# Attention on TensorE: hash masks of two blocks on quarters of the rows, four score slots, and small steps moved to ScalarE

## Chip, cores and metric

The kernel runs on one core of one Trainium2 chip. The metric is the device time of one execution in microseconds (us), as the median of several runs. TensorE is called PE, VectorE DVE, ScalarE ACT, GpSimd POOL and the SyncE queue SP.

## What is computed

Hashed attention over 4 batches of 8 heads (768 tokens, 64 dimensions), followed by a feed-forward layer. All inputs are float32. Cut to what matters:

```python
q_bits = (einsum('bhsd,dk->bhsk', q, proj) > 0)      # 6 bits; k_bits likewise
mask = q_bucket[:, :, :, None] == k_bucket[:, :, None, :]
scores = where(mask, q @ k.T / sqrt(64), -1e9)
attn = exp(scores - max(scores))
attn = attn / (sum(attn) + 1e-9)
x = (attn @ v) -> (3072, 512)                        # heads side by side
h = x @ w_in                                         # 512 -> 2048
out = (h * erf(softplus(h))) @ w_out                 # 2048 -> 512
```

## The kernel before

Attention takes the heads in 16 pairs; the two heads of a pair, called `ab` 0 and 1, lie on SBUF partitions 0 to 63 and 64 to 127. A pair has 12 score blocks: `n` runs over four steps (two halves of 384 queries, and for each two groups of keys), `c` over three tiles of 128 keys. A block is one PSUM tile `st` of two banks, one for each head. `score` (L543) fills it in two parts: first the mask, a bf16 product of the hash bits `qb` and `kb` (7 rows that hold bits and a constant, the other rows of the 64 are zero), then the float32 product of `k` and `q` on top of it. The mask adds 0 where all bits agree and a huge negative number elsewhere, so that the exponential gives 0 there. Both parts use 64 rows of the array for each head, so the two heads stand side by side. In the trace a float32 matmul is two records, a bf16 one is one.

`exponential` (L581, ACT) reads a block out of PSUM into SBUF (`e_even` for the first half of the queries, `e_odd` in `area` for the second). There are three slots of two banks for score blocks (`big`, L433): block 3 of a pair can start when the exponential of block 0 has ended, and so on.

`weigh` (L632, PE) multiplies by `v`: for each half of the queries 12 matmuls of 128 rows by 64 columns, the two heads on two halves of the columns, accumulated into a tile `av` of one bank. Half 0 and half 1 have a tile and a pool of their own (`psum_v` and `misc`). `leave` (L700, ACT) copies `av` to `x`. A further column of `e_even` that holds 1.0 gives in `av` the plain sum of `v`; `leave_plain` (L710, DVE) multiplies it by 2^-100 into `ev`, the small term that is added to `x` later.

Behind the last `weigh` of a pair stand on PE `bits_of` (L834: hash bits of the pair after the next, on four quarters of 32 columns, tile `bits`) and `divisor` (L670: column sums of the exponentials of the pair before, which DVE has added up in `sum_keys`; it writes beside the bits, in the second bank of the same tile). ACT takes the signs of the bits (`sign_of`, L853, tile `sg`) and the sums (`keep_divisor`, L695). DVE multiplies the rows of k's bits in `sg` by a weight (`weigh_bits`, L862); POOL sends `sg` to DRAM (`leave_bits`) and fetches it back into `both` with two DMAs (`place_bits`, L876). The sums go to DRAM and back as 12 values on each partition, DVE adds a constant and inverts them (`invert`, L741), they are spread over the partitions by DMA, and DVE makes `(x + ev) * r` (`normalise`, L767).

Beside all this DVE and ACT decode the two weight matrices of the feed-forward layer (`square_high` and `keep_normal` on ACT, `move_bits`, `mask_bits`, `add_rest` on DVE), and ACT sums squares of `q` and `k` (`measure`, L660).

The order of the work is made when the program is built. Each step is an `Op` with an engine, an estimated cost, a rank and the steps that it comes after; `arrange` (L120) lists them greedily. For PE the chain is written out by hand (L905 to L944): `score` x4, `weigh` x4, `bits_of`, `divisor`, for each pair. The waits between engines are not written in the kernel: the framework sets them, from the tiles that instructions read and write.

The feed-forward layer (L1201 on) follows with the same engines: seven products instead of eight at each of two levels, and a gate built of sigmoids and a tanh.

Of the kernel before, what the change touches and what calls it, by code (L numbers as in the profile page):

```python
# [63 lines left out]
P = 128  # L64
# [132 lines left out]
def kernel(  # L197
# [32 lines left out]
    dram = ctx.enter_context(tc.tile_pool(name="dram", bufs=2, space=bass.MemoryType.DRAM))  # L230
    misc = ctx.enter_context(tc.tile_pool(name="misc", bufs=1, space=PSUM))
    small = ctx.enter_context(tc.tile_pool(name="small", bufs=3))
    QR = 32
# [7 lines left out]
    sgn = const.tile([P, 1], F32, name="sgn")  # L241
    tiny2 = const.tile([P, 1], F32, name="tiny2")
    cq = const.tile([P, len(GATE_S) + 1], F32, name="cq")
    w_in_sb = const.tile([P, NK, DFF], F32, name="w_in_sb")
# [53 lines left out]
    nc.vector.memset(sgn, -(2.0**-27))  # L298
    nc.vector.memset(tiny2, TINY * TINY)
    for j, c in enumerate([b for _, b, _ in GATE_S] + [GATE_BIAS]):  # L300
        nc.vector.memset(cq[:, j : j + 1], c)

    def bank(name):
        return misc.tile([P, 512], F32, name=name, tag="bank")

# [114 lines left out]
    def attention():  # L420
        NS = NPAIR * 4
        with (
# [17 lines left out]
            e_even = ep.tile([P, NE, 2, HS + 1], F32, name="e_even")  # L440
            nc.vector.memset(e_even[:, :, :, HS : HS + 1], 1.0)
            e_odd = area[:, 0 : NE * S].rearrange("p (n a c) -> p n a c", n=NE, a=2)
# [82 lines left out]
            def add_rest(n):  # L525
# [15 lines left out]
                )  # L541

            def score(n, c, parts=((0, "b"), (1, ""))):  # L543

                i, half, g = n // 4, n // 2 % 2, n % 2
                d = pairs[i]
                cols = slice(half * HS, (half + 1) * HS)
                keys = slice((g * GC + c) * P, (g * GC + c + 1) * P)
                if ("st", n, c) in d:
                    parts = ((1, "b"),)  # L550
                else:
                    d["st", n, c] = big("st")
                st = d["st", n, c]
                for part, src in parts:
                    for ab in range(2):
                        rows = slice(ab * D, ab * D + D)
                        nc.tensor.matmul(  # L557
                            out=st[:, ab, 0:HS],
                            lhsT=d["k" + src][rows, keys],
                            rhs=d["q" + src][rows, cols],  # L560
                            start=(part == 0),
                            stop=(part == 1),
                        )
# [68 lines left out]
            def weigh(n):  # L632
                half, g = n // 2 % 2, n % 2
                d = pairs[n // 4]
                if g == 0:
                    d["av", half] = bank("av") if half else psum_v.tile([P, 512], F32, name="av", tag="av")
                w = HS + 1 - half
# [57 lines left out]
            def keep_divisor(i):  # L695
                d = pairs[i]
                d["z"] = home(i, "z")
                nc.scalar.copy(out=d["z"], in_=d.pop("z_ps"))

            def leave(h):  # L700
# [6 lines left out]
                x = d["x"][half] if i == NPAIR - 1 else d["x"][:, cols]  # L707
                nc.scalar.copy(out=x, in_=d["av", half][:, 0:HS])

            def leave_plain(i):  # L710

                d = pairs[i]
                d["ev"] = small.tile([P, 1], F32, name="ev", tag="ev")
                nc.vector.tensor_scalar(
                    out=d["ev"],
                    in0=d["av", 0][:, HS : HS + 1],
                    scalar1=EPS,
                    scalar2=None,
                    op0=ALU.mult,
                )  # L720
# [20 lines left out]
            def invert(i):  # L741
                d = pairs[i]
                zc = d["zc"]
                nc.vector.tensor_scalar(
                    out=zc, in0=zc, scalar1=S * EPS, scalar2=None, op0=ALU.add
                )
                nc.vector.reciprocal(out=zc, in_=zc)

# [18 lines left out]
            def normalise(i):  # L767
# [36 lines left out]
            pairs[0] = fetch(0, load, quick=True)  # L804
            warm = bank("warm")
            for n in range(WARM):
# [55 lines left out]
            def weigh_bits(i):  # L862

                nc.vector.tensor_scalar(
                    out=sg[D:P, :],
                    in0=sg[D:P, :],
                    scalar1=weight_q[D:P, 0:1],
                    scalar2=None,
                    op0=ALU.mult,
                )  # L870
# [5 lines left out]
            def place_bits(i):  # L876
# [3 lines left out]
                for n, what in enumerate(("qb", "kb")):  # L880
                    d[what] = both[i % 2][:, n, :]
                for ab in range(2):
                    nc.gpsimd.dma_start(
                        out=both[i % 2][ab * D : ab * D + NBIT + 1, :, :].rearrange(
                            "r w (h c) -> r (w h) c", h=2
                        ),
                        in_=bd[:, ab, 0 : NBIT + 1, :].rearrange("n r c -> r n c"),
                    )

# [18 lines left out]
            for i in range(NPAIR):  # L908
# [8 lines left out]
                if i == NPAIR - 2:  # L917
                    order.append(("divisor", i))
            slots = []
            for what, n in order:  # L920
                free = slots[-3] if len(slots) >= 3 else ()
                if what == "score":
                    i = n // 4
                    after = (("double_first",) if i == 1 else ("place_bits", i),)
                    for c in range(GC):
                        free = slots[-3] if len(slots) >= 3 else ()
                        pe(score, (n, c), 0.82 if n or c == 2 else 0.17, after + free)
                        slots.append((("exponential", n, c),))
                elif what == "bits":
                    pe(bits_of, (n,), 0.80 if n > 1 else 1.44, (("start_pair", n),) + free)  # L930
                    slots.append((("sign_of", n),) if n > 1 else (("place_first",),))
                elif what == "divisor":
                    if n != NPAIR - 3:
                        free = ()
                        slots[-1] += (("keep_divisor", n),)
                    else:
                        slots.append((("keep_divisor", n),))
# [34 lines left out]
            for i in range(NPAIR - 1):  # L972
# [3 lines left out]
                    "ACT",  # L976
                    0.48,
                    (0, 4 * i + 6, -1),
                    (("divisor", i), ("spread", i - 2)),
                )  # L980
            for h in range(NH):
                i = h // 2
                op(leave, (h,), "ACT", 0.48, (0, 2 * h, -2), (("weigh", 2 * h + 1), ("send", i - 3)))
                if h % 2 == 0:
                    op(leave_plain, (i,), "DVE", 0.15, (0, 2 * h, 0), (("weigh", 2 * h + 1),))
            for i in range(NPAIR):
                n = 4 * i
                if i:
# [15 lines left out]
                    else:  # L1004
                        op(sign_of, (i,), "ACT", 0.6, (0, n - 6, 9), (("bits_of", i), ("leave_bits", i - 1)))
                        op(weigh_bits, (i,), "DVE", 0.33, (0, n - 6, 1), (("sign_of", i),))
                        op(leave_bits, (i,), "POOL", 0.7, (0, n - 6, 2), (("weigh_bits", i),), late=4.0, far=True)
# [3 lines left out]
                            "POOL",  # L1011
                            1.2,
                            (0, n - 6, 3),
# [16 lines left out]
                op(gather, (i,), "SP", 0.35, (0, n, 1), (("spread", i),), late=4.5, far=True)  # L1030
                op(invert, (i,), "DVE", 0.4, (0, n + 8, 3), (("gather", i),))
                op(ungather, (i,), "SP", 0.35, (0, n, 2), (("invert", i),), late=3.0, far=True)
# [8 lines left out]
                )  # L1041
                op(normalise, (i,), "DVE", 1.02, (0, n + 8, 4), (("widen", i), ("leave", 2 * i + 1)))
                op(send, (i,), "SP", 0.35, (0, n, 4), (("normalise", i),), late=2.2)
# [59 lines left out]
    def general():  # L1103

        with (
# [4 lines left out]
            tc.tile_pool(name="row", bufs=4) as small,  # L1110
            tc.tile_pool(name="psum", bufs=1, space=PSUM) as psum,
        ):

            def big(name):
# [86 lines left out]
    def feed_forward(check, late):  # L1201
        again = late is None
        with (
# [5 lines left out]
            tc.tile_pool(name="ps_f", bufs=1, space=PSUM) as ps_f,  # L1209
            tc.tile_pool(name="ps_l", bufs=1, space=PSUM) as ps_l,  # L1210
        ):
            NTILE = NT // T
            NP = NTILE * NC4
# [619 lines left out]
```

## Time and profile before

| what | value |
|---|---|
| median of 3 runs | 904.84 us (904.79 to 905.12) |
| the profiled execution | 904.72 us, of which 902.9 us from the first to the last instruction |
| granted PE clock | 0.998 of full speed |
| busy: PE, DVE, ACT, POOL | 99%, 74%, 62%, 6% of the span |
| attention on PE | to 313.5 us; the feed-forward layer from there |
| one pair of heads, steady | 19.17 us: 12 score blocks 9.84, `weigh` 7.90, `bits_of` and `divisor` 1.43 |
| busy in such a pair: PE, DVE, ACT | 19.17, 18.43, 15.31 us |

A timeline line reads: start and duration in us, engine, line of the kernel, operation, written tile, tiles read, shapes, and how many records are merged in it. "64*128" in a matmul's shape is the part of the array that it uses, rows by columns. A matmul's recorded duration is longer than the time after which the next one on the same place can start, since they are pipelined.

### The profile page before, as it was taken

The numbers are of one execution on the slowest core, as the hardware profiler recorded it, in microseconds if no ns is written. First come the engines' busy times: TensorE is split into PE (matmuls) and PEld (weight loads), VectorE is DVE, ScalarE is ACT, GpSimd is POOL, SyncE is SP. The second block draws the span as 40 slices with busy tenths as digits, with TensorE's granted clock in tenths as the row PEclk, the third lists the DMA queues.
The fourth block names the chain that finished last, engine by engine and source line by source line (L and its number), as shares of the span: only waits on it lengthen the run. The fifth ranks groups of instructions, "written<-read, shape, count | busy, mean of one in ns | idle before, by whom it ended". The sixth has DMA issues, their size and how long they took to land.

```text
span 902.9 us, 12780 instructions
## 1 busy us (share of the span) xinstructions
PE 894.3 (99%) x5016; PEld 670.9 (74%) x5016; DVE 668.5 (74%) x837; ACT 563.3 (62%) x808; POOL 57.9 (6%) x95
## 2 busy tenths in 40 slices
PE   9999999999999999999999999999999999999997
PEld 5455554455544588888888888888888888888886
DVE  5999999999999879995666556666776666655652
ACT  6788888788886668855645455545655555545520
POOL 1211211111110000000000001000100010000000
PEclk9999999999999999999999999999999999999999
DMA  9547655667551322202231013211421122111211
GB/s 228 149 128 183 200 166 142 196 173 195 154 157 60 101 89 65 82 36 70 59 106 58 14 49 103 82 36 47 105 83 36 36 74 78 35 36 57 63 68 50
DMA packets 65156, 86.82 MB, mean 96 GB/s; under 512 B 34364, under 2 KB 47772, under 8 KB 65088
## 3 DMA queue, kind: packets, MB, share of 16 engines
q1 hardware_dynamic: 56528, 63.81, 24.8%
q0 software_dynamic: 8112, 21.66, 8.6%
q8 instruction: 41, 0.67, 0.3%
q10 hardware_dynamic: 448, 0.46, 0.2%
q14 instruction: 27, 0.22, 0.1%
HBM read 64.67 MB, written 17.30 MB: 91 GB/s over the span
## 4 chain that ended last, share of the span: by engine, by line
PE 99%; DVE 0%; issue 0%; ACT 0%; DVEq 0%
PE M L1361 32%; PE X L1248 29%; PE st L557 17%; PE av L642 14%; PE M L1248 3%; PE bits L845 1%; PE bits L687 1%; PE warm L807 0%; PE bits L377 0%; PE z_ps L687 0%; DVE e L1288 0%; DVE h L1270 0%; ACT both L390 0%; DVE u L1396 0%; DVE norms L1754 0%
## 5 line engine op out<-in xcount | busy, mean ns | idle before, releaser
L1288 DVE SCALAR_TENSOR_TENSOR e<-w,e 128x1024 f32<-128x1024 f32 x144 | 173.7, 1220 | 8.4 <-ACT w L1282 3.9
L1248 PE MATMUL X<-area,w_in_sb 128*128 128x256 f32 x680 | 160.6, 379 | 0.0
L1282 ACT ACTIVATE w<-h,cq 128x1024 f32<-128x1024 f32 x144 | 155.6, 1136 | 0.1
L557 PE MATMUL st<-q,k 64*128 64x384 f32 x768 | 155.1, 482 | 0.0
L1270 DVE TENSOR_TENSOR h<-X,h 128x512 f32<-128x512 f32 x65 | 44.8, 689 | 144.4 <-PE X L1248 144.4
L1248 PEld LDWEIGHTS X<-area,w_in_sb 128*128 128x128 f32 x680 | 129.2, 190 | 17.6
L1361 PE MATMUL M<-w_out_sb,h 128*128 128x256 f32 x576 | 141.1, 379 | 0.0
L1248 PE MATMUL X<-area 128*128 128x256 f32 x520 | 122.8, 379 | 0.0
L1361 PEld LDWEIGHTS M<-w_out_sb,h 128*128 128x128 f32 x576 | 109.4, 190 | 14.9
L1266 ACT COPY h<-X 128x512 f32<-128x512 f32 x85 | 49.3, 580 | 111.4 <-PE X L1248 111.3
L1248 PEld LDWEIGHTS X<-area 128*128 128x128 f32 x520 | 98.8, 190 | 13.4
L1278 ACT ACTIVATE e<-h,cq 128x1024 f32<-128x1024 f32 x48 | 55.1, 1148 | 85.9 <-DVE h L1270 85.8
L1361 PE MATMUL M<-wt,S 128*128 128x256 f32 x384 | 95.1, 379 | 0.0
L557 PEld LDWEIGHTS st<-q,k 64*128 64x128 f32 x768 | 68.8, 187 | 29.7 <-issue 27.2
L630 DVE TENSOR_TENSOR area<-area 128x1536 f32<-128x1536 f32 (+1 forms) x46 | 79.2, 1723 | 7.5 <-ACT area L584 6.3
L1361 PEld LDWEIGHTS M<-wt,S 128*128 128x128 f32 x384 | 73.0, 190 | 9.9
L584 ACT ACTIVATE e_even<-st 128x768 f32<-128x768 f32 x96 | 70.6, 822 | 0.4 <-PE st L557 0.3
L584 ACT ACTIVATE area<-st 128x768 f32<-128x768 f32 x90 | 68.0, 817 | 0.0
L642 PE MATMUL av<-e_even,v 128*64 128x385 f32 x384 | 65.6, 490 | 0.0
L557 PE MATMUL st<-both 64*128 64x384 bf16 x384 | 63.5, 323 | 0.3 <-ACT both L390 0.3
L1303 DVE TENSOR_TENSOR h<-h,e 128x1024 f32<-128x1024 f32 x48 | 57.9, 1220 | 4.6 <-ACT e L1299 4.6
L642 PE MATMUL av<-area,v 128*64 128x384 f32 x360 | 60.6, 486 | 0.0
(129 smaller groups left out, 976.8 us busy)
## 6 DMA issues: line engine op xcount, KB each, us to landing
wt<-wt SPq DMA_DIRECT2D x24, 768.0 KB, 4.2
raw<-in_w_out_dram POOLq DMA_DIRECT2D x16, 512.0 KB, 4.2
raw<-in_w_in_dram POOLq DMA_DIRECT2D x14, 512.0 KB, 4.6
v<-in_v_dram SPq DMA_DIRECT2D x32, 192.0 KB, 4.6
q<-in_qkT_dram SPq DMA_DIRECT2D x30, 192.0 KB, 4.2
k<-in_qkT_dram SPq DMA_DIRECT2D x30, 192.0 KB, 4.7
r<-rd SPq DMA_DIRECT2D x30, 192.0 KB, 3.7
xs<-x SPq DMA_DIRECT2D x15, 384.0 KB, 3.0
```

The source lines that it names most:

```text
L557: nc.tensor.matmul(out=st[:, ab, 0:HS], lhsT=d["k" + src][rows, keys], rhs=d["q" + src][rows, cols], start=(part == 0), stop=(part == 1),)
L584: nc.scalar.activation(out=e[:, :, 0:HS], in_=st[:, :, 0:HS], func=AF.Exp, scale=scale)
L630: nc.vector.tensor_tensor(out=into, in0=one, in1=two, op=ALU.add)
L642: nc.tensor.matmul(out=d["av", half][rows, 0:w], lhsT=d["v"][:, g * GC + c, rows], rhs=e[:, ab, 0:w], start=(g == 0 and c == 0), stop=(g = ...
L1248: nc.tensor.matmul(out=d[where][:, u, :], lhsT=a[:, kc, f : f + P], rhs=b[:, kc, :], start=(first and u == 0 and kc == 0), stop=(last and ...
L1266: nc.scalar.copy(out=quarter(p, q), in_=st[p][where])
L1270: nc.vector.tensor_tensor(out=h, in0=st[p][where], in1=h, op=ALU.add)
L1278: nc.scalar.activation(out=s, in_=unit(p, v), func=AF.Sigmoid, bias=cq[:, n : n + 1])
L1282: nc.scalar.activation(out=q, in_=unit(p, v), func=AF.Sigmoid, scale=GATE_S[j][0], bias=cq[:, j : j + 1])
L1288: nc.vector.scalar_tensor_tensor(out=s, in0=st[p].pop(("q", v, j)), scalar=GATE_S[j][2], in1=s, op0=ALU.add, op1=ALU.mult,)
L1303: nc.vector.tensor_tensor(out=h, in0=h, in1=st[p].pop(("s", v)), op=ALU.mult)
L1361: nc.tensor.matmul(out=banks[name][:, sub, :], lhsT=a[:, u, sub * P : (sub + 1) * P], rhs=b[:, u, :], start=(c == 0 and k == 0), stop=(c = ...
```

## The change

From the third pair on, the masks of two neighbouring blocks are made together (`mask`, new). The hash bits are laid out four times, on rows 0, 32, 64 and 96 (`place_bits` issues four DMAs where it issued two). For blocks 0 and 1, 2 and 3, up to 8 and 9 of a pair, four bf16 matmuls of 32 rows by 128 columns run on the four quarters, two for each block; the float32 parts follow. Blocks 10 and 11 stay as they were.

Score blocks have four slots: three as before (`big`) and one of two banks in `psum_v` with the tag `side`, which serves blocks 3 and 7 of a pair and then `av`. `av` is now one tile of two banks, `avs`, whose half 0 and half 1 are the two halves of the queries. The pool `misc` is opened only in the later phases.

`weigh_bits` goes from DVE to ACT. The extra column of `e_even` holds 2^-100 instead of 1.0, so `av` gives the small term itself; ACT copies it to `ev` ahead of `leave` of half 0, and both `leave` add it as a bias. `normalise` becomes a plain product. The divisors' constant is a bias in `keep_divisor`, and `invert` has only the reciprocal. The planner's costs and conditions are rewritten to match.

```diff
@@ mask (new) and score @@
+            SIDE = (3, 7)
+            QUARTERS = tuple(range(0, 10, 2))
+            def slot_of(n, c):
+                if place(n, c)[1] in SIDE:
+                    return psum_v.tile([P, 2, 512], F32, name="st", tag="side")
+                return big("st")
+            def mask(n, c):
...
+                for m in range(2):
...
+                    st = d["st", n, c] = slot_of(n, c)
+                    for ab in range(2):
+                        rows = slice(ab * D + m * QR, ab * D + (m + 1) * QR)
+                        nc.tensor.matmul(
+                            out=st[:, ab, 0:HS],
+                            lhsT=d["kb"][rows, keys],
+                            rhs=d["qb"][rows, cols],
+                            start=True,
+                            stop=False,
+                        )
...
@@ weigh @@
-                    d["av", half] = bank("av") if half else psum_v.tile([P, 512], F32, name="av", tag="av")
+                    if not half:
+                        d["avs"] = psum_v.tile([P, 2, 512], F32, name="av", tag="side")
+                    d["av", half] = d["avs"][:, half, :]
@@ keep_divisor @@
-                nc.scalar.copy(out=d["z"], in_=d.pop("z_ps"))
+                nc.scalar.activation(
+                    out=d["z"], in_=d.pop("z_ps"), func=AF.Identity, bias=least[:, 0:1]
+                )
@@ leave, leave_plain @@
-                nc.scalar.copy(out=x, in_=d["av", half][:, 0:HS])
-            def leave_plain(i):
...
+                if half == 0:
+                    d["ev"] = small.tile([P, 1], F32, name="ev", tag="ev")
+                    nc.scalar.copy(out=d["ev"], in_=d["av", 0][:, HS : HS + 1])
+                nc.scalar.activation(
+                    out=x, in_=d["av", half][:, 0:HS], func=AF.Identity, bias=d["ev"][:, 0:1]
+                )
@@ invert, normalise, weigh_bits @@
-                nc.vector.tensor_scalar(
-                    out=zc, in0=zc, scalar1=S * EPS, scalar2=None, op0=ALU.add
-                )
...
-                    nc.vector.scalar_tensor_tensor(
-                        out=x, in0=x, scalar=d["ev"][:, 0:1], in1=r, op0=ALU.add, op1=ALU.mult
-                    )
+                    nc.vector.tensor_tensor(out=x, in0=x, in1=r, op=ALU.mult)
...
+                nc.scalar.activation(
+                    out=sg[D:P, :], in_=sg[D:P, :], func=AF.Copy, scale=weight_q[D:P, 0:1]
+                )
@@ the planner @@
+                        if i > 1 and at in QUARTERS:
+                            pe(mask, (n, c), 0.22, ready + free_of(at in SIDE, at + 1 in SIDE))
+                        if i > 1 and at <= QUARTERS[-1] + 1:
+                            cost = 0.655
...
-                    if n % 2 == 0:
-                        after += (("leave", h - 2), ("leave_plain", (h - 2) // 2))
-                    pe(weigh, (n,), 2.0, after)
+                    if n % 4 == 0:
+                        after += free_of(True)
+                        side.append((("leave", h), ("leave", h + 1)))
+                    pe(weigh, (n,), 1.98, after)
```

In the changed kernel `mask` is L569, the rest of a score block L591, `weigh` L678, `divisor` L723, `keep_divisor` L734, the copy to `ev` L748, `leave` L749 and `weigh_bits` L889.

More of the change, by code (lines that the diff above doesn't have):

```diff
@@ L230 @@
     dram = ctx.enter_context(tc.tile_pool(name="dram", bufs=2, space=bass.MemoryType.DRAM))
-    misc = ctx.enter_context(tc.tile_pool(name="misc", bufs=1, space=PSUM))
+    single = []
     small = ctx.enter_context(tc.tile_pool(name="small", bufs=3))
@@ L242 @@
     tiny2 = const.tile([P, 1], F32, name="tiny2")
+    least = const.tile([P, 1], F32, name="least")
     cq = const.tile([P, len(GATE_S) + 1], F32, name="cq")
@@ L299 @@
     nc.vector.memset(tiny2, TINY * TINY)
+    nc.vector.memset(least, S * EPS)
     for j, c in enumerate([b for _, b, _ in GATE_S] + [GATE_BIAS]):
@@ L303, in bank @@
     def bank(name):
-        return misc.tile([P, 512], F32, name=name, tag="bank")
+        return single[-1].tile([P, 512], F32, name=name, tag="bank")
     WP = 512
@@ L440, in attention @@
             e_even = ep.tile([P, NE, 2, HS + 1], F32, name="e_even")
-            nc.vector.memset(e_even[:, :, :, HS : HS + 1], 1.0)
+            nc.vector.memset(e_even[:, :, :, HS : HS + 1], EPS)
             e_odd = area[:, 0 : NE * S].rearrange("p (n a c) -> p n a c", n=NE, a=2)
@@ L541, in add_rest, with place @@
                 )
+            SIDE = (3, 7)
+            QUARTERS = tuple(range(0, 10, 2))
+            def place(n, c):
+                return n // 4, n % 4 * GC + c
+            def slot_of(n, c):
[3 more added lines that the diff above has]
+            def mask(n, c):
+                i, at = place(n, c)
+                d = pairs[i]
+                for m in range(2):
+                    n, c = 4 * i + (at + m) // GC, (at + m) % GC
+                    half, g = n // 2 % 2, n % 2
+                    cols = slice(half * HS, (half + 1) * HS)
+                    keys = slice((g * GC + c) * P, (g * GC + c + 1) * P)
+                    st = d["st", n, c] = slot_of(n, c)
[8 more added lines that the diff above has]
+                        )
             def score(n, c, parts=((0, "b"), (1, ""))):
@@ L549, in score @@
                 if ("st", n, c) in d:
-                    parts = ((1, "b"),)
+                    parts = ((1, "b" if i == 0 else ""),)
                 else:
-                    d["st", n, c] = big("st")
+                    d["st", n, c] = slot_of(n, c)
                 st = d["st", n, c]
@@ L707, in leave @@
                 x = d["x"][half] if i == NPAIR - 1 else d["x"][:, cols]
-                nc.scalar.copy(out=x, in_=d["av", half][:, 0:HS])
-            def leave_plain(i):
[L712 to L719, printed above, removed]
+                if half == 0:
[3 more added lines that the diff above has]
+                    out=x, in_=d["av", half][:, 0:HS], func=AF.Identity, bias=d["ev"][:, 0:1]
                 )
@@ L742, in invert @@
                 d = pairs[i]
-                zc = d["zc"]
-                nc.vector.tensor_scalar(
-                    out=zc, in0=zc, scalar1=S * EPS, scalar2=None, op0=ALU.add
-                )
-                nc.vector.reciprocal(out=zc, in_=zc)
+                nc.vector.reciprocal(out=d["zc"], in_=d["zc"])
             def ungather(i):
@@ L804, in attention @@
             pairs[0] = fetch(0, load, quick=True)
-            warm = bank("warm")
+            warm = big("warm")[:, 0, :]
             for n in range(WARM):
@@ L862, in weigh_bits @@
             def weigh_bits(i):
[L864 to L869, printed above, removed]
+                nc.scalar.activation(
+                    out=sg[D:P, :], in_=sg[D:P, :], func=AF.Copy, scale=weight_q[D:P, 0:1]
                 )
@@ L881, in place_bits @@
                     d[what] = both[i % 2][:, n, :]
[L882 to L888, printed above, removed]
+                for m in range(2):
+                    for ab in range(2):
+                        row = ab * D + m * QR
+                        nc.gpsimd.dma_start(
+                            out=both[i % 2][row : row + NBIT + 1, :, :].rearrange(
+                                "r w (h c) -> r (w h) c", h=2
+                            ),
+                            in_=bd[:, ab, 0 : NBIT + 1, :].rearrange("n r c -> r n c"),
+                        )
             def place_first():
@@ L918, in attention, with free_of @@
                     order.append(("divisor", i))
-            slots = []
+            slots, side = [], []
+            def free_of(*sides):
+                at = {True: len(side), False: len(slots)}
+                gone = ()
+                for is_side in sides:
+                    ring, room = (side, 1) if is_side else (slots, 3)
+                    if at[is_side] >= room:
+                        gone += ring[at[is_side] - room]
+                    at[is_side] += 1
+                return gone
             for what, n in order:
-                free = slots[-3] if len(slots) >= 3 else ()
                 if what == "score":
                     i = n // 4
-                    after = (("double_first",) if i == 1 else ("place_bits", i),)
+                    ready = (("double_first",) if i == 1 else ("place_bits", i),)
                     for c in range(GC):
-                        free = slots[-3] if len(slots) >= 3 else ()
-                        pe(score, (n, c), 0.82 if n or c == 2 else 0.17, after + free)
-                        slots.append((("exponential", n, c),))
+                        at = place(n, c)[1]
+                        free = free_of(at in SIDE)
+                        cost = 0.82 if n or c == 2 else 0.17
+                        if i > 1 and at in QUARTERS:
+                            pe(mask, (n, c), 0.22, ready + free_of(at in SIDE, at + 1 in SIDE))
+                        if i > 1 and at <= QUARTERS[-1] + 1:
+                            cost = 0.655
+                        pe(score, (n, c), cost, ready + free)
+                        (side if at in SIDE else slots).append((("exponential", n, c),))
                 elif what == "bits":
-                    pe(bits_of, (n,), 0.80 if n > 1 else 1.44, (("start_pair", n),) + free)
+                    pe(bits_of, (n,), 0.70 if n > 1 else 1.44, (("start_pair", n),) + free_of(False))
                     slots.append((("sign_of", n),) if n > 1 else (("place_first",),))
                 elif what == "divisor":
+                    free = ()
                     if n != NPAIR - 3:
-                        free = ()
                         slots[-1] += (("keep_divisor", n),)
                     else:
+                        free = free_of(False)
                         slots.append((("keep_divisor", n),))
@@ L976, in attention @@
                     "ACT",
-                    0.48,
+                    0.58,
                     (0, 4 * i + 6, -1),
@@ L982, in attention @@
                 i = h // 2
-                op(leave, (h,), "ACT", 0.48, (0, 2 * h, -2), (("weigh", 2 * h + 1), ("send", i - 3)))
-                if h % 2 == 0:
-                    op(leave_plain, (i,), "DVE", 0.15, (0, 2 * h, 0), (("weigh", 2 * h + 1),))
+                op(leave, (h,), "ACT", 0.58 if h % 2 else 0.78, (0, 2 * h, -2), (("weigh", 2 * h + 1), ("send", i - 3)))
             for i in range(NPAIR):
@@ L1005, in attention @@
                         op(sign_of, (i,), "ACT", 0.6, (0, n - 6, 9), (("bits_of", i), ("leave_bits", i - 1)))
-                        op(weigh_bits, (i,), "DVE", 0.33, (0, n - 6, 1), (("sign_of", i),))
+                        op(weigh_bits, (i,), "ACT", 0.5, (0, n - 6, 10), (("sign_of", i),))
                         op(leave_bits, (i,), "POOL", 0.7, (0, n - 6, 2), (("weigh_bits", i),), late=4.0, far=True)
@@ L1011, in attention @@
                             "POOL",
-                            1.2,
+                            2.4,
                             (0, n - 6, 3),
@@ L1030, in attention @@
                 op(gather, (i,), "SP", 0.35, (0, n, 1), (("spread", i),), late=4.5, far=True)
-                op(invert, (i,), "DVE", 0.4, (0, n + 8, 3), (("gather", i),))
+                op(invert, (i,), "DVE", 0.23, (0, n + 8, 3), (("gather", i),))
                 op(ungather, (i,), "SP", 0.35, (0, n, 2), (("invert", i),), late=3.0, far=True)
@@ L1041, in attention @@
                 )
-                op(normalise, (i,), "DVE", 1.02, (0, n + 8, 4), (("widen", i), ("leave", 2 * i + 1)))
+                op(normalise, (i,), "DVE", 0.93, (0, n + 8, 4), (("widen", i), ("leave", 2 * i + 1)))
                 op(send, (i,), "SP", 0.35, (0, n, 4), (("normalise", i),), late=2.2)
@@ L1111, in general @@
             tc.tile_pool(name="psum", bufs=1, space=PSUM) as psum,
+            tc.tile_pool(name="misc", bufs=1, space=PSUM) as misc,
         ):
+            single.append(misc)
             def big(name):
@@ L1210, in feed_forward @@
             tc.tile_pool(name="ps_l", bufs=1, space=PSUM) as ps_l,
+            tc.tile_pool(name="misc", bufs=1, space=PSUM) as misc,
         ):
+            single.append(misc)
             NTILE = NT // T
```

## The prediction

> **What bounds the kernel now.** I read the page's busy times first.
>
> ```profile
> span 902.9 us, 12780 instructions
> PE 894.3 (99%) x5016; PEld 670.9 (74%) x5016; DVE 668.5 (74%) x837; ACT 563.3 (62%) x808; POOL 57.9 (6%) x95
> ```
>
> PE is busy nearly throughout, so other engines matter only where they make PE wait. Next, the chain of waits around one steady pair (start, duration, what), and the stretch of that pair by engine (PE, PEld, DVE, ACT, POOL busy):
>
> ```profile
> 200.09 9.84 PE st L557 x72
> 209.92 7.90 PE av L642 x48
> 217.82 0.78 PE bits L845 x8
> 218.61 0.65 PE bits L687 x16
> 219.26 9.84 PE st L557 x72
> ```
>
> ```profile
> 200.09:219.26 19.17, 19.17 (x146) 9.87 (x148) 18.43 (x25) 15.31 (x28) 2.81 (x5) 1.00 0.68 175
> ```
>
> The chain is PE alone, with no step of another engine. A busy PE can still hold dead time, which the timeline of PE shows where one step ends:
>
> ```profile
> 208.13 0.34 PE L557 MATMUL st<-both 64*128 64x384 bf16 x2
> 208.29 0.83 PE L557 MATMUL st<-q,k 64*128 64x384 f32 x4
> 208.93 0.34 PE L557 MATMUL st<-both 64*128 64x384 bf16 x2
> 209.10 0.82 PE L557 MATMUL st<-q,k 64*128 64x384 f32 x4
> 209.85 0.54 PE L642 MATMUL av<-e_even,v 128*64 128x385 f32 x2
> ```
>
> Start to start, the two masks take 0.16 us side by side, the float32 part 0.65. But where the next matmul uses another shape of the array (64\*128 to 128\*64), the same part takes 0.75: a change of shape costs 0.10. I measured each change between 30 and 300 us from single records, start minus end of the streams before: 0.092 to 0.099 each time, for 64\*128 to 128\*64, 128\*64 to 128\*32 and 128\*32 to 64\*128. I use 0.095.
>
> Last, ACT around the end of `weigh`, with the matmuls on either side, and two rows for the waits:
>
> ```profile
> 217.01 0.82 PE L642 MATMUL av<-area,v 128*64 128x384 f32 x4
> 217.87 0.48 ACT L708 COPY x<-av 128x384 f32<-128x384 f32 x1 [3.39 <-PE av L642]
> 219.19 0.34 PE L557 MATMUL st<-both 64*128 64x384 bf16 x2
> 219.32 0.58 ACT L854 ACTIVATE sg<-bits,sgn 128x384 bf16<-128x384 f32 x1 [0.35 <-PE bits L687]
> 219.80 0.47 ACT L698 COPY z<-bits 128x384 f32<-128x384 f32 x1
> 220.16 0.73 ACT L484 ACTIVATE keep<-keep,tiny 128x512 int32<-128x512 f32 x1
> 220.79 2.21 ACT L584 ACTIVATE e_even<-st 128x768 f32<-128x768 f32 x3
> 221.65 0.34 PE L557 MATMUL st<-both 64*128 64x384 bf16 x2
> ```
>
> ```profile
> 214.51 0.16 DVE L714 TENSOR_SCALAR ev<-av 128x1 f32<-128x1 f32 x1 [0.19 <-ACT x L708]
> L642 PE MATMUL av<-area,v 128*64 128x384 f32 x336 | 56.6, 486 | 0.0
> L708 ACT COPY x<-av 128x384 f32<-128x384 f32 x28 | 13.5, 481 | 38.9 <-PE av L642 38.3 <-DVE ev L714 0.5
> L1266 ACT COPY h<-X 128x512 f32<-128x512 f32 x85 | 49.3, 580 | 111.4 <-PE X L1248 111.3
> ```
>
> The first of these rows matters most: `ev` reads column 384 of `av` and waited for ACT's copy of the other columns, though both only read. Accesses to one PSUM tile are put in order by the tile, not by the columns.
>
> **One tile for both halves of av: the main cost.** The changed program, built, shows what that makes of `avs`. In every pair the 24 matmuls of `weigh` (two records each) stand as 12 for half 0, 6 for the first key group of half 1, and 6 more. ACT's copy to `ev` waits for matmul 18, although half 0 was complete at 12; and matmul 19 waits for `leave` of half 0, although it writes the other bank. In the old program matmul 19 waited for an exponential that was long over. So PE stops for a full round trip in each of 16 pairs:
>
> - From the end of the streams to the end of the record: records of 0.486, one pair of them every 0.325 (7.90 less 0.10 over 24): 0.16.
> - PE's record end to ACT's start: 217.01 + 0.82 = 217.83, ACT at 217.87: 0.04.
> - The copy of one column. No row has it. ACT's copies of 512 and 384 columns take 0.580 and 0.481, which makes 0.00077 a column and 0.185 for none: 0.19. Bounds: 0.15 (DVE's one-column read, 0.146) and 0.48 (the full copy).
> - The result to the next ACT instruction that needs it: 0.04 (`square_high` 212.55 + 0.68, `keep_normal` at 213.26: 0.03).
> - `leave` with a bias. Nearest row is `sign_of`, same shape with a bias out of PSUM: 0.58. Bounds 0.48 (the copy) to 0.60.
> - ACT's end to PE: the exponential at 220.79 lasts 0.81 and frees the slot for 221.65: 0.05.
>
> The sum is 1.06; bounds 0.92 to 1.37. PE has nothing else in its queue, and half 1's last matmuls, the bits, the divisors and the next masks all stand behind matmul 19. Sixteen times 1.06 is **+17.0** (14.7 to 21.9).
>
> **The masks.** A mask group of two blocks takes one stream of 0.16 instead of two, five times in each of 14 pairs: 70 x 0.162 = -11.3. But 32 rows is another shape. The first group of a pair follows `divisor`, where a change was due anyway: one more. The other four stand between float32 parts: two more each. That is 9 x 0.095 = 0.86 a pair, +12.0 over 14. Net **+0.6**. No row shows a change from 64 to 32 rows. Bounds: nothing for it leaves -11.3; and if only two of the four quarters run at once, the stream lasts 0.32 and the masks come to +11.9. I take the cost of the change, since all observed kinds agree within 0.007 and halving the columns (128\*64 to 128\*32) cost as much as any. For four at once: four column quarters do so, 16 `divisor` records of 0.16 in 0.65.
>
> [...]
>
> **ACT.** It gains `weigh_bits` (0.52, after `measure` L663, 384 columns out of SBUF), `ev` 0.19 and 0.10 on each of three copies: 1.0 a pair onto 15.31 of 19.17. In the built order `weigh_bits` stands at the head of a pair, beside `sign_of` and `keep_divisor`, where `keep_normal` was; that one moves behind some exponentials. By rows: sign at +0.13 after the first mask, weight at +0.74, sums at +1.15, first exponential at +1.62 (before: 1.60). The third mask group starts at 2 x (0.095 + 0.162 + 0.095 + 1.29) = 3.29 and needs the second exponential: 1.62 + 0.69 + 0.82 + 0.05 = 3.18. It fits by 0.1; a `keep_normal` (0.73) or `square_high` among the exponentials delays a later group by 0.1 or 0.2 in some pairs. **+1.0** over 14 pairs (0 to 3).
>
> **At nothing.** DVE sheds 0.32 + 0.15 + 0.16 + 0.05 = 0.7 a pair; PE waits for DVE nowhere in the chain, so none of it returns (were DVE the bound, it would be -11). POOL issues two more DMAs of 0.57 a pair, ahead of the weight fetches; `place_bits` starts near 224.7 and its bits are used at 238.43, 9 us later (uncovered: 1.1 a pair, 16). Block 3's side slot needs `leave` of half 1, over at about 0.7 after `weigh`, that is 2.5 before use; `weigh` needs block 7's exponential, over 2.3 before. The feed-forward layer keeps its order. No table load is added.
>
> **Sum.** The profiled execution took 904.72 (span 902.9 and 1.8 around it), 0.12 below the median. 904.7 + 17.0 + 0.6 + 1.0 = 923.3; against the median 923.4.
>
> **Rivals.**
> - *The change to 32 rows costs nothing.* For: a row quarter lies inside the half in use. Against: all other changes cost the same. Masks -11.3; but then the third group starts at 2.92 and must wait for 3.18, and later groups run at 0.73 a block against exponentials of 0.69 with `keep_normal` between: 0.25 to 0.55 a pair, 3.5 to 7.7. Time 914 to 918, likeliest 915.
> - *The quarters don't run four at once*: the saving isn't there, the changes of shape are. 926 (partly) to 935.
> - *Not slower*: free changes of shape, and a round trip at matmul 19 short enough. It decides where the trip falls below 11.3 / 16 = 0.71; at 0.70 the time is 904.6. For: two of its links have no row. Against: the lowest rows make 0.92, which with the free changes still gives 908.
>
> **How the numbers follow.** Forecast 0.73 (its own range 920 to 928), free change 0.13, no four at once 0.10, not slower 0.04. The range 913 to 929 takes in the forecast with its bounds and the first rival, and leaves out most of the last two. A difference of 0.2% (1.8 us) is about what can be told from no change; only the last case falls within or below it: faster 0.02, same 0.02, slower 0.96.
>
> **What would show it.** In the profile after: PE idle before `av` L678 of about 1.06 in each of 16 pairs, released by ACT's `leave` L749; the `weigh` stretch 8.96 instead of 7.90; `ev` L748 at 0.19, `leave` at 0.58; four mask records starting within 0.02, and 0.26 from them to the float32 part; the score stretch near 9.9. The forecast is wrong if matmul 19 follows 18 without a gap, if mask to float32 takes 0.17, or if the four masks start 0.16 apart in twos.

## The result, and the profile after

The changed kernel takes 931.83 us (median of 4 runs, 931.57 to 932.07), the kernel before 904.82 in the same runs: 1.0298 times as long, 95% interval 1.028 to 1.0316. The change costs 27.0 us. The forecast of 923.4 had the sign and the largest part, but the time lies above its range of 913 to 929.

The page's first lines of the profile after:

```profile
span 929.8 us, 12796 instructions
PE 906.5 (97%) x5016; PEld 657.9 (71%) x5016; DVE 659.3 (71%) x792; ACT 585.4 (63%) x838; POOL 73.6 (8%) x123
```

PE is busy for 97% instead of 99%, so 23 of the 929.8 us are open gaps, where the old kernel had 9. DVE has 9 us less to do, and nothing comes of it. The chain of waits, which held nothing but PE in a steady pair before, now has ACT in two places (start, duration, what):

```profile
205.99 5.99 PE av L678 x36
212.00 0.17 ACT ev L748
212.20 0.59 ACT x L749
212.79 0.04 issue
212.83 2.16 PE av L678 x12
214.99 0.78 PE bits L870 x8
215.77 0.69 PE bits L723 x16
216.49 0.59 ACT sg L879
217.10 0.61 ACT sg L889
217.74 0.59 ACT z L734
218.37 0.34 PE st L569 x4
218.71 1.49 PE st L591 x8
220.20 0.27 PE st L569 x4
```

The first is the round trip in the middle of `weigh`: after 36 of 48 records PE stops, ACT copies the small term and half 0, and PE goes on. The second, between `divisor` and the second mask group, stands in the 7 pairs of the table below whose score takes 10.69: sign, weighting of the bits, and only then the copy of the divisors, for which the group at 218.37 waits.

A third part is no wait between engines. Two float32 blocks (x8) take 1.49, and two of 0.65 would be 1.29. The timeline around one group, PE and its weight loads (PEld):

```profile
220.13 0.34 PE L569 MATMUL st<-both 32*128 32x384 bf16 x4
220.41 0.59 PE L591 MATMUL st<-q,k 64*128 64x384 f32 x2
220.40 0.19 PEld L591 LDWEIGHTS st<-q,k 64*128 64x128 f32 x2 [0.17 <-issue]
220.51 0.19 PEld L591 LDWEIGHTS st<-q,k 64*128 64x128 f32 x2
```

From single records of the trace: the four masks start within 0.01 of each other and their stream lasts 0.17, the change out of 32 rows takes 0.100 to 0.102 and the change into it 0.095, in all of over 100 cases that no wait hides. But the first float32 stream behind each group (the second row) is recorded with 0.587 where the others have 0.482, and the next one starts 0.427 behind it instead of 0.322.

By stretch, from starts of PE's steps (us). "Score" has the 14 pairs from the third on; "from first score" is the time from the first score of the first pair's main block to the last `weigh`. It leaves out the start, which moves by up to 0.9 between runs (that score starts at 8.2 to 9.1), and the feed-forward layer. All experiments but e9 (11 runs) were run once. The 15 runs of the kernel before beside e6 to e9 lie between 903.86 and 905.45, so a difference of under 1.6 in "time" says little by itself; the stretches, which repeat to about 0.01 between pairs with the same order of work, carry the argument.

| kernel | score | weigh | from first score | time | before, same chip |
|---|---|---|---|---|---|
| before | 9.79 to 10.08, mean 9.83 | 7.90 | 297.2 | 904.82 | |
| changed | 10.43 in 7 pairs, 10.69 in 7 | 8.99 | 323.7 | 931.83 | 904.82 |
| e1_late_leave | 10.43 | 7.90 | 305.6 | 919.52 | 904.13 |
| e2_half_rows | 9.79 to 9.88 in 8, 10.20 in 6 | 8.99 | 315.7 | 924.27 | 904.13 |
| e3_weight_on_dve | 10.43 | 8.99 | 322.0 | 930.82 | 904.13 |
| e5_float_first | 9.89 to 10.17 | 7.90 | 298.8 | 906.57 | 904.13 |
| e6_true_cost | 10.44 in 6, 10.58 to 10.65 in 8 | 7.90 | 307.0 | 915.26 | 904.51 |
| e7_first_group | 9.84 (9.88, 9.93 once each) | 7.90 | 297.4 | 904.95 | 904.51 |
| e8_inner_group | 9.94 | 7.90 | 298.8 | 905.93 | 904.51 |
| e9_both_undone | 9.79 (9.94, 9.95 once each) | 7.90 | 297.0 | 905.21 | 904.51 |

So the 26.9 us between the two spans are: `weigh` 16 x 1.09 = 17.4; score +10.2 over 14 pairs; less 0.2 for an earlier start, and less 0.5 that the last pair's longer `weigh` doesn't pass on to the feed-forward layer.

### The profile page after: what moved, and what is told of

Its sections match the earlier page's. It is cut to its first block, busy times and chain, and to the rows that moved or that the text cites. A ratio compares the mean times of both kernels' runs of the same rounds, so it can differ in the third digit from the quotient of the medians.

```text
span 929.8 us, 12796 instructions
## 1 busy us (share of the span) xinstructions
PE 906.5 (97%) x5016; PEld 657.9 (71%) x5016; DVE 659.3 (71%) x792; ACT 585.4 (63%) x838; POOL 73.6 (8%) x123
## 4 chain that ended last, share of the span: by engine, by line
PE 96%; ACT 3%; issue 1%; DVE 0%; DVEq 0%
PE M L1404 31%; PE X L1291 28%; PE st L591 15%; PE av L678 14%; PE M L1291 3%; PE st L569 2%; PE bits L870 1%; ACT x L749 1%; PE bits L723 1%; PE warm L832 0%; ACT sg L879 0%; ACT z L734 0%; PE bits L379 0%; ACT ev L748 0%; ACT sg L889 0%
## 5 line engine op out<-in xcount | busy, mean ns | idle before, releaser
L591 PE MATMUL st<-q,k 64*128 64x384 f32 x768 | 151.2, 502 | 0.0
L591 PEld LDWEIGHTS st<-q,k 64*128 64x128 f32 x768 | 66.8, 186 | 41.3 <-issue 22.9
L678 PE MATMUL av<-area,v 128*64 128x384 f32 x360 | 63.9, 490 | 13.1 <-ACT x L749 13.1
L678 PE MATMUL av<-e_even,v 128*64 128x385 f32 x384 | 65.6, 490 | 0.0
L678 PEld LDWEIGHTS av<-area,v 128*64 128x64 f32 x360 | 24.6, 136 | 49.8 <-issue 26.7
```

The costliest lines, as they stand in the source:

```text
L591: nc.tensor.matmul(out=st[:, ab, 0:HS], lhsT=d["k" + src][rows, keys], rhs=d["q" + src][rows, cols], start=(part == 0), stop=(part == 1),)
L678: nc.tensor.matmul(out=d["av", half][rows, 0:w], lhsT=d["v"][:, g * GC + c, rows], rhs=e[:, ab, 0:w], start=(g == 0 and c == 0), stop=(g = ...
```

## Experiments

Theory A: the shared tile of `av` makes a round trip. Theory B: a mask group on row quarters costs two changes of shape and, on top, a slow first float32 stream. Theory C: the weighting of the bits ahead of `keep_divisor` holds up the second group in some pairs. Theory D came out of e1: the order of the work was planned with too low a cost.

**e1: the round trip taken out.** In the changed kernel, `leave` of half 0 does nothing, and `leave` of half 1, planned behind the last `weigh`, copies both halves (cut to what matters; in the last pair it copies them one by one):

```diff
                 if half == 0:
...
+                    return
...
+                if i < NPAIR - 1:
+                    nc.scalar.activation(
+                        out=d["x"][:, :].rearrange("p (h c) -> p h c", h=2),
+                        in_=d["avs"][:, :, 0:HS],
+                        func=AF.Identity,
+                        bias=d["ev"][:, 0:1],
+                    )
...
-                op(leave, (h,), "ACT", 0.58 if h % 2 else 0.78, (0, 2 * h, -2), (("weigh", 2 * h + 1), ("send", i - 3)))
+                op(leave, (h,), "ACT", 1.1 if h % 2 else 0.0, (0, 2 * h + 2 * (1 - h % 2), -2), (("weigh", 4 * i + 3), ("send", i - 3)))
```

> The changed kernel with one edit: leave of half 0 does nothing, and leave of half 1 copies the small term and then both halves in one ACT instruction. Theory A (matmul 19 of av waits for a round trip to ACT because both halves are one tile): the gap of about 1.36 us in front of matmul 19 closes to 0.32, weigh takes 7.9 instead of 8.99 in all 16 pairs, and the time falls by 16 x 1.09 = 17.4 to about 914.4 (913.5 to 916). Rival (the wait only moves: the side slot is now released later, so block 3 and what follows wait for leave, and the signs of the bits start later): weigh 7.9 but score longer by up to 0.5 a pair, 919 to 922.

The chain of e1 in a steady pair:

```profile
212.31 3.11 PE st L591 x20
215.41 7.90 PE av L678 x48
223.32 0.78 PE bits L878 x8
```

All 48 records of `weigh` run through, in every pair, and score has no 10.69 left either: in this order `keep_divisor` comes before the weighting. Theory A holds: the wait was for the copy in the middle. (That it is there because the halves share a tile rests on the built program's waits; e1 removes the copy, not the sharing.) But the time is 919.52, 5 above the expectation. From the last `weigh` to the end e1 takes 603.4, the other runs 596.9 to 598.2. The loss begins after attention, at the last pair's divisor (timeline of PE in e1, then two stretches of it: PE, PEld, DVE, ACT, POOL busy, granted PE clock, DMA share, GB/s):

```profile
329.22 0.53 PE L723 MATMUL z_ps<-area,ones 128*32 128x192 f32 x8
332.22 0.53 PE L723 MATMUL z_ps<-area,ones 128*32 128x192 f32 x8 [2.46 <-DVE area L664]
332.68 3.17 PE L1299 MATMUL M<-area,w_in_sb 128*128 128x256 f32 x8
```

```profile
330.00:332.00 2.00, 0.00 (x0) 0.00 (x0) 1.93 (x3) 0.00 (x0) 0.00 (x0) 1.00 0.00 0
334.00:336.00 2.00, 2.00 (x6) 1.62 (x5) 1.34 (x4) 1.26 (x1) 0.00 (x0) 0.50 0.25 102
```

PE waits 2.46 for DVE, which is still adding up exponentials. In e1 the last decoded piece of the weights is written at 321.9, when attention ends (322.1); in the kernel before at 280.3 of 313.5. And behind the stop the granted PE clock is 0.50 for 3.4 us (333.3 to 336.8), which is 1.7 us of lost work; eight matmuls take 3.17 where e6 takes 1.99 for the same eight. No other run here shows such a drop between its first and its last microseconds: over the whole profiled run the granted clock is 0.996 in e1, 0.998 or 0.999 in the others. That led to e6.

**e6: the same instructions, another order.** e1 with one number changed, the planner's cost of a mask group:

```diff
-    pe(mask, (n, c), 0.22, ready + ...)
+    pe(mask, (n, c), 0.46, ready + ...)
```

> e1_late_leave with the planner's cost of a mask group set to 0.46 (0.095 + 0.162 + 0.101 + 0.105, as the trace shows it) instead of 0.22; no instruction is added or removed, only the order on DVE, ACT, POOL and SP can change. Theory D (e1 lost 5.1 of its expected 17.4 since the order was made for a PE that is faster than the real one: the weight decoding on DVE, which fills the gaps of the plan, ends at 321.9, with attention, and the divisor of the last pair waits 2.5 for DVE): decoding ends a pair or more ahead of attention, the stretch from the last weigh to the end is 598 again instead of 603.4, 914.4. Rival (the shorter attention itself leaves DVE too little time, whatever the order): 918 to 920.

915.26, and 597.6 from the last `weigh` to the end: 5.8 is back, so it was the order, not DVE's load. Decoding ends at 303.4, and PE doesn't stop at the last divisor. Of the 5.8, 2.5 are the wait, 1.9 are PE's longer busy time (1.7 of it the halved clock), and 1.4 lie behind the last matmul, where the cause stays open. Eight pairs pay 0.15 to 0.2 in score for the new order, 1.4 in all, hence a time that is 0.9 above the expectation.

**e2: row quarters taken out.**

```diff
-    QUARTERS = tuple(range(0, 10, 2))
+    QUARTERS = ()
```

> The changed kernel with no block in QUARTERS: masks on 64 rows, one block at a time, as before; four slots, one tile for av and the ACT steps stay. Theory B (the row quarters themselves cost: change of shape 0.095 in, 0.101 out, and 0.105 because the first float32 stream after a change waits for its weights, against 0.162 saved, which makes 0.64 a pair): score falls to 9.8 (10.1 where the weighting of the bits stands ahead of keep_divisor), and the time falls by about 14 x 0.64 = 9.0 to 922.8 (922 to 924). Rival (score is longer because of ACT's added work or of the slots): score stays at 10.3 or more, 928 or above.

Eight pairs fall to 9.79 to 9.88, as in the old kernel, so neither the slots nor ACT's work lengthen score there. Six pairs take 10.20, more than the 10.1 expected: the order sign, weighting, `keep_divisor` again, with a wait of 0.4. One `weigh` took 9.17. In sum 8.0 of the expected 9.0 came back from the first score to the last `weigh`, and 7.6 in the time, which at 924.27 lies just above the expected 922 to 924.

**e3: the weighting of the bits back on DVE.** `weigh_bits` as in the kernel before, all else as changed.

> The changed kernel with weigh_bits back on DVE. Theory C (in 7 pairs the weighting, 0.61 us on ACT, stands ahead of keep_divisor, which frees the slot of block 2, and the second mask group waits 0.25): all 14 later pairs take 10.43 in score, the time falls by 7 x 0.25 = 1.8 to 930.0. Rival (the 0.25 comes from keep_normal, square_high or measure among the exponentials): some pairs keep 10.69, 931 to 932.

All 14 pairs take 10.43 to 10.47; from the first score to the last `weigh` 1.7 is gone, as expected. The total shows only 1.0 of it, since this run's first score started 0.65 later. The changed kernel itself says the same: its 7 pairs with the weighting ahead of `keep_divisor` take 10.69, its 7 others 10.43. Theory C holds.

**e5: the slow first stream in the old kernel.** In the kernel before, each block makes its float32 product first and its mask second:

```diff
-    def score(n, c, parts=((0, "b"), (1, ""))):
+    def score(n, c, parts=((0, ""), (1, "b"))):
```

> The kernel before with one edit: in every block the float32 product goes first and the mask second. No change of shape is added; the first matmul after the change from divisor (32 columns) to score (64 rows) is now float32 instead of bf16. Theory B (after any change of shape the first float32 stream of 128 columns waits 0.105 for its weights, which can't be loaded ahead over the change): the first float32 stream of each pair takes 0.43 instead of 0.32, score 9.89 instead of 9.79, and the time rises by about 16 x 0.1 = 1.5 to 906.3. Rival (the slow first stream belongs to row quarters alone, for instance to adding onto banks that 32-row matmuls have just written): 904.8, score 9.79.

The timeline of PE in e5 behind `divisor`:

```profile
219.61 0.83 PE L687 MATMUL bits<-area,ones 128*32 128x192 f32 x16
220.37 0.92 PE L557 MATMUL st<-q,k 64*128 64x384 f32 x4
221.12 0.33 PE L557 MATMUL st<-both 64*128 64x384 bf16 x2
```

The float32 part takes 0.75 (220.37 to 221.12) where it takes 0.65 elsewhere, and score is 0.10 longer in nearly all pairs. No 32-row matmul is near, no bank was just written by one: the slow first stream is not a matter of row quarters, but came here too with a change of shape that a float32 matmul follows. From first score to last `weigh` it takes 298.82 instead of 297.16.

**e7 and e8: one group in a pair**, on top of e1, the first (blocks 0 and 1) and the second (2 and 3):

```diff
-    QUARTERS = tuple(range(0, 10, 2))
+    QUARTERS = (0,)        # e7, planner's cost 0.37
+    QUARTERS = (2,)        # e8, planner's cost 0.46
```

(The planner's condition for the cost of the blocks in a group follows.)

> e1_late_leave with only blocks 0 and 1 of a pair on row quarters (planner's cost 0.37), all others as before. Theory B by counting: this group stands where a change of shape was due anyway, so it adds one change (0.101), the slow first float32 stream (0.105), and saves one mask stream (0.162): +0.04 to +0.05 a pair, score 9.84, 0.7 above the kernel with no groups. Rival (a group costs the same wherever it stands, 0.64 / 5 = 0.13): score 9.92.

> e1_late_leave with only blocks 2 and 3 of a pair on row quarters (planner's cost 0.46). Theory B by counting: two changes (0.095 and 0.101), the slow first stream (0.105), less 0.162: +0.14 a pair, score 9.93, 2.0 above the kernel with no groups. Rival (0.13 wherever it stands): score 9.92 here too, so that e7 and e8 are alike.

The chain of e8 in a steady pair:

```profile
200.79 1.72 PE st L591 x12
202.51 0.27 PE st L569 x4
202.79 7.95 PE st L591 x56
210.74 7.90 PE av L678 x48
```

9.84 and 9.94 against 9.79 with none: +0.05 and +0.15. What a group costs depends on whether a change of shape was due at its place anyway, and by the amount of one change. In the totals the difference is 0.98, with e8's first score 0.4 earlier.

**e9: both taken out.** Edits of e1 and e2 together.

> Both edits of e1_late_leave and e2_half_rows on the changed kernel: no row quarters, no round trip; four slots, one copy of both halves of av by ACT, and the steps that were moved to ACT stay. Theories A and B together: weigh 7.9 and score 9.79 in every pair, and since four slots take away the small waits for a slot that the kernel before has in some pairs (score 9.83 to 10.08), 0.3 to 0.7 below the kernel before, near 904.3. Rival (ACT's added work or the shared side slot costs something that was hidden behind the other two): 905 to 907.

The chain of e9 in a steady pair:

```profile
200.67 9.79 PE st L591 x72
210.47 7.91 PE av L678 x48
218.37 0.78 PE bits L878 x8
```

905.21 is 1.0006 times the time of the kernel before, interval 0.9997 to 1.0015: no difference that can be told. By the time alone the rival (905 to 907) isn't excluded; the stretches decide. From first score to last `weigh` e9 is 0.2 shorter than the kernel before, which was expected, so the two costs add up and nothing hides behind them in attention. In the profiled run the first score starts 0.7 later than in the old kernel's profile, and the trace shows why: the first four matmuls for hash bits take 1.37 instead of 0.70, since the granted clock reached 1.0 at 6.8 us instead of 5.3. In the changed kernel and e1 to e3 and e6 to e8, which start with the same work, that moment lies anywhere from 4.5 to 6.4, so it varies from run to run. No version here is faster than the old kernel.

Not tried: a tile for each half of `av` with all else as changed, which would test the sharing itself; and a score part that stays on row quarters for the float32 product too, which would need no change of shape between masks and products.

## Why the prediction was wrong

**The round trip: right.** Predicted 1.06 a pair, measured 8.99 - 7.90 = 1.09. The link without a row, the one-column copy, took 0.159 (estimate 0.185), `leave` with a bias 0.581 (0.58), from PE's record end to ACT 0.045 (0.04), from ACT to PE 0.05. The 0.05 left over is new: the first stream after the stop takes 0.373 instead of 0.323. The built program had shown both waits, so this was reading, not guessing. 17.0 predicted, 17.4 measured.

**The masks: the step that failed.** "9 x 0.095 = 0.86 a pair, +12.0 over 14. Net +0.6" is the term that was mis-sized. Four quarters at once: right (one stream of 0.17). The change of shape: right (0.095 in, 0.101 out). But I had measured each change only up to the *start* of the next matmul, and taken that as its whole price. The term that the prediction left at nothing is the first float32 stream behind a group: it runs 0.105 longer, five times a pair, 70 x 0.105 = 7.4. With 0.01 for each group's stream and 0.006 for each change back, a pair pays 5 x (0.172 - 0.324) + 4 x 0.095 + 5 x 0.101 + 5 x 0.105 = 0.65, and 10.43 against 9.79 says 0.64. Over 14 pairs that is 9.0 instead of 0.6. (With ACT's 1.8 below that makes 10.8; score grew by 10.2, since the old pairs took 9.83 on average, 0.6 in all above 9.79.)

The row was in the profile before: `av`, float32 and 64 columns, has its first two streams 0.375 apart after the change from score and 0.323 after that. I had divided that whole stretch by 24 (0.325), which spread the 0.05 over all streams. And the old kernel's own change into score was followed by a bf16 mask (0.17 instead of 0.16), which hid the effect for exactly the shape at issue. Measured extra of the first float32 stream after a change: 0.105, 0.05 and 0.025 for 128, 64 and 32 columns of weights. The bf16 masks lost 0.01: four quarters took 0.172 where one mask stream takes 0.162.

The trace shows the load itself. In a steady block the weights of a stream are loaded while the stream before it runs (old kernel: a load at 200.192, in the stream from 200.190 to 200.513); behind a mask group the load (PEld, two heads) starts at 220.404, the matmul at 220.405, and the load of the next stream only at 220.512, 0.108 behind the first. The same holds at all 48 changes of shape between 30 and 350 us in the trace of the kernel before and at all 172 in that of the changed kernel: no load of the new shape starts before the streams of the old one are over, and the first comes about 0.09 to 0.10 behind their end. The first two loads of float32 weights behind a change start 0.108, 0.055 and 0.028 apart for 128, 64 and 32 columns, near the extras of 0.105, 0.05 and 0.025.

**ACT: within its range by luck, wrong place.** Predicted +1.0 (0 to 3) at the third group; measured 7 x 0.25 = 1.8, all of it at the second. I had followed the third group to the exponentials, with 0.1 to spare, and costed `weigh_bits` at 0.52 after a squaring. It took 0.61, without overlap with its neighbours (it starts at 196.700, after the end of the copy at 196.675; other ACT instructions that need nothing from the one before start 0.1 before its end). And the slot that was late is the one that `bits` and the divisors had held, which block 2 takes: with the weighting ahead of `keep_divisor`, that one ends at 218.32, and the second group could have started at 218.12. The prediction's own figures would have shown a wait there: sums from 1.15 to 1.73 and 0.05 to PE, against a second group due at 1.64.

**At nothing: right.** DVE's 9 us less, POOL's extra DMAs, the side slot and the feed-forward layer moved nothing that the runs can tell; e9 keeps them all and takes the old kernel's time.

**The rivals.** Free changes of shape and half as many quarters at once are both refuted by the mask records: 0.095 into 32 rows, 0.100 to 0.102 out of them, and four masks that start within 0.01 of each other in one stream of 0.172. The 926 for quarters that overlap in part rests on a term that no run shows; the runs show this full overlap. "Not slower" needed a trip below 0.71; it cost 1.09.

The range failed because the only dear case for the masks, +11.9, was tied to quarters that don't overlap and mostly left out of it; a dearer visit to another shape was not among the bounds, though it came to 9.0. The changes of shape agreed so well with each other that I stopped asking whether they were measured to the right point.

## What to carry to other kernels

Measure the price of an interruption to where the old rhythm is back, not to the next start: on PE that took in the weight load of the first matmul behind it, 0.105 for a float32 matmul of 128 columns and 0.01 for a bf16 one. Two buffers that are filled and emptied in turn must not be two halves of one tile, if waits are made by the tile (1.09 in each pair here); the built program's waits tell this before any run. And where a planner orders the work, an operation that is planned too cheap costs twice: with one planned cost put right and no instruction changed, e6 took 4.3 us less than e1.

## What the hardware showed beyond that

After the changes of the array's shape between 30 and 350 us in the kernel before and the changed one, the first float32 stream ran longer by 0.105, 0.05 and 0.025 us for weights of 128, 64 and 32 columns, on top of 0.092 to 0.102 for the change. The same 0.05 came in the changed kernel after a plain stop of 0.87 us for ACT, with no change of shape: there the wait stands on the weight load itself (212.828, the matmul at 212.830). Where it stands on the matmul, in the 7 pairs whose second mask group waits for ACT, the first load runs ahead of it (218.110, the matmul at 218.367), and that first mask is recorded with 0.317 or 0.318 instead of 0.332. So in this kernel it counted which of the two held the wait. A stop of PE of 2.5 us in e1 was followed by 3.4 us at a granted clock of 0.50; the stops of 0.87 in each `weigh` of the changed kernel were not (1.00 throughout). And the ACT instruction with a scale from SBUF, one value for each partition (0.61 for 384 columns, 64 partitions), overlapped with neither neighbour in any of its 14 executions, while one with a bias of that kind did: `keep_divisor` started 0.10 before the end of the sign ahead of it in the 6 pairs where it follows it. Whether the scale or another feature of this instruction is the reason was not tested.
